# Weights through SyncE's queue in 2 KB rows, with staging and casts, in place of a software DMA that casts

## The chip, the cores and the metric

One core of one Trainium2 chip. The metric is the device time of one execution in microseconds (us); the kernel before has a median of 257.8 us (3 runs, 257.32 to 258.01). Ratios are of one kernel's fast runs over the other's fast runs of the same rounds, so they are not quite the ratio of the medians that are quoted. A profile's span is about 1.8 us shorter than the time of the same run (258.8 for 260.65).

## The reference

Attention with 16 query heads and 4 key heads, and then a gated MLP with a spatial mix; 8 batches of 384 positions.

```python
scores = (q @ k^T) / sqrt(64);  attn = softmax(scores);  x = attn @ v   # x: 8 x 384 x 1024
h = max(x @ w_in, 0)                       # w_in: 1024 x 1024 float32
u, v = h[..., :512], h[..., 512:]
v_n = (v - mean(v)) / sqrt(var(v) + 1e-6)
v_s = w_spatial @ v_n + b_spatial          # w_spatial ~ 0.01/384, b_spatial = 1
out = (u * v_s) @ w_out                    # w_out: 512 x 1024 float32
```

The weights are shared by all batches: they are read once, while the first batch is worked on.

## The kernel before

The kernel is a list of steps (`FIRST` for batches 0 to 2, `STEADY`, `LAST`), and every engine runs its steps in the order of the list. In the code, `S` is a product of scores, `E` its exponential, `X` the product with v, `V` the product x @ w_in for the half v, `G,..,gu` the same for the half u, `Tw` the transposes of w_spatial, `cq`/`ck`/`cv`/`cws` casts of loaded data to 16 bits (last letter: v = VectorE, s = ScalarE, p = GpSimd), and `dk`/`dq` DMA transposes.

Row `32*g + r` of `w_in16` and of `xT` holds feature `256*g + 32*kc + r`, because the program lets the X products of each group g of heads write to their own 32 partitions (128\*32 in the page's line of X). This layout matters below. Weights are loaded by a software DMA from GpSimd, which casts on the way (in the trace each w_in load writes 256 KB for its 512 KB of float32):

```python
def load_w_in(part, g):                                   # eight of these, 512 KB of float32 each
    c0, c1 = part * DH, (part + 1) * DH
    nc.gpsimd.dma_start(
        w_in16[32 * g : 32 * (g + 1), :, c0:c1],
        moe_w_in[g * G * D : (g + 1) * G * D, c0:c1].rearrange("(kc r) n -> r kc n", r=32),
    )

def load_w_out(h):                                        # two of these
    nc.gpsimd.dma_start(w_out16[:, 2 * h : 2 * h + 2, :], ...)

def v_mm(b, st, k0=0, k1=NKT):                            # "V": needs all eight kc of w_in
    for kc in range(k0, k1):
        nc.tensor.matmul(held["pv", b, st], xT[b][:, kc, st * P : (st + 1) * P],
                         w_in16[:, kc, DH:DFF], start=(kc == 0), stop=(kc == NKT - 1))
# ... all loads of q, k, v and w_spatial: nc.sync.dma_start with the 128 partitions outermost
```

The softmax here doesn't subtract the row's maximum and nothing guards it: scores larger than these inputs give would overflow.

Of the kernel before, what the change touches and what calls it, by code (L numbers as in the profile page):

```python
# [17 lines left out]

FIRST = """
lk,0,0,2 lq,0,0,0,1,s cq,0,0,0,1,0,v ck,0,0,s Tk,0,0 cq,0,0,0,1,1,s lk,0,2,4 Tq,0,0,0 lq,0,1,0,1  # L20
lq,0,0,1,3 lq,0,1,1,3 cq,0,1,0,1,1,p tq,0,0,0,v tk,0,0,s S,0 cq,0,1,0,1,0,v ck,0,1,v E,0 S,0
lwi,0,1,3 cq,0,0,1,3,0,p lwi,0,1,0 cq,0,1,1,3,0,p Tk,0,1 lk,1 lv,0 Tq,0,1,0 tk,0,1,v tq,0,1,0,v S,0
lq,1,0 cq,0,0,1,3,1,v E,0 E,0 lq,1,1 S,0 Tq,0,0,1 S,0 S,0 Tq,0,0,2 cq,0,1,1,3,1,p tq,0,0,1,v
Tq,0,1,1 tq,0,1,1,v S,0 ck,1,1,p tq,0,0,2,v E,0 lwi,0,1,2 lwi,0,1,1 ck,1,0,p S,0 E,0 cv,0,p E,0
X,0,0,2 S,0 lv,1 lws,0 Tq,0,1,2 S,0 S,0 lbi,0 Tkk,1 rv,0,0 E,0 lk,2 S,0 X,0,0,0 X,0,0,1 lq,2,0
lq,2,1 E,0 cq,1,0,0,1,1,p E,0 E,0 E,0 S,0 cq,1,0,1,3,0,p cq,1,0,1,3,1,p cq,1,0,0,1,0,p tq,0,1,2,v
tkk,1,v cq,1,1,0,1,0,p S,0 E,0 xm,0,0,1 X,0,1,2 xm,0,0,0 X,0,1,0 X,0,1,1 S,0 S,0 V,0,0,0,4 V,0,0,4,8
rv,0,1 S,0 S,0 E,0 E,0 E,0 E,0 cq,1,1,0,1,1,s xm,0,1,0 xm,0,1,1 Tqq,1,0 tqq,1,0,0,v V,0,1,0,4
ru,0,0,v cq,1,1,1,3,0,v tqq,1,0,1,v cv,1,v E,0 E,0 S,0 S,0 E,0 X,0,2,0 X,0,2,2 X,0,2,1 lwi,0,0,2
cws,0,0 cws,0,2 cq,1,1,1,3,1,p cws,0,1 lwi,0,0,0 lwo,0,1 cq,2,0,0,3,0,p lwi,0,0,3 lwi,0,0,1  # L30
cq,2,0,0,3,1,p cq,2,1,0,3,0,p ck,2,1,p lwo,0,0 ck,2,0,p cq,2,1,0,3,1,p E,0 rl,0,2 S,0 re,0,2 E,0 S,0
xm,0,2,1 Tqq,1,1 E,0 xm,0,2,0 V,0,1,4,8 Tw,0,0,2 Tw,0,2,3 S,0 S,0 tqq,1,1,0,s ru,0,1,v tw,0,0,2
V,0,2,0,4 V,0,2,4,8 bs,0,0 bs,0,1 ru,0,2,v tqq,1,1,1,v E,0 tw,0,2,3 bs,0,2 S,0 E,0 E,0 S,0 X,1,0,2
rl,1,0 X,1,0,0 X,1,0,1 Tqq,1,2 S,0 re,1,0 S,0 xm,1,0,0 xm,1,0,1 V,1,0,0,4 E,0 dq,2,0 dk,2 V,1,0,4,8
S,0 rs,0 tqq,1,2,0,v nm,0,2 E,0 tqq,1,2,1,v nm,0,0 nm,0,1 ru,1,0,v G,0,gs,0,0,0,1 S,0 G,0,gs,2,0,0,1
dq,2,1 lq,3,1 lk,3 E,0 mk,0,gs,0,v G,0,gs,0,1,0,1 S,0 lv,2 lq,3,0 mk,0,gs,2,v G,0,gs,2,1,0,1 E,0 E,0
sa,0,0 sa,0,1 sa,0,2 sa,0,3 S,0 cq,3,1,0,3,1,p cq,3,1,0,3,0,p X,1,1,2 cq,3,0,0,3,0,p cq,3,0,0,3,1,p
X,1,1,1 X,1,1,0 E,0 rl,1,1 re,1,1 ck,3,0,p xm,1,1,0 xm,1,1,1 G,0,gu,0,0,0 S,0 G,0,gu,0,0,1 E,0 S,0
mk,0,gu,0,v G,0,gu,2,0,0 S,0 E,0 E,0 G,0,gu,0,1,0 S,0 G,0,gu,2,0,1 S,0 G,0,gu,0,1,1 mk,0,gu,2,v E,0
E,0 E,0 bs,1,0 G,0,gu,2,1,0 S,0 G,0,gu,2,1,1 S,0 gt,0,0 E,0 X,1,2,0 gt,0,2 gt,0,3 gt,0,1 X,1,2,2  # L40
cv,2,v E,0 S,0 S,0 V,1,1,0,4 rl,1,2 V,1,1,4,8 S,0 G,0,go,0,0,0 G,0,go,0,0,1 mk,0,go,0,v S,0 re,1,2
E,0 E,0 G,0,go,0,1,0 E,0 G,0,go,0,1,1 S,0 E,0 xm,1,2,0 oc,0,1,v oc,0,0,v E,0 X,2,0,2 X,1,2,1 rl,2,0
xm,1,2,1 re,2,0 ru,1,1,s X,2,0,0 X,2,0,1 S,0 S,0 xm,2,0,0 G,1,w12,2,0,0 G,1,w12,2,0,1 S,0 S,0
ck,3,1,s E,0 E,0 mk,1,w12,2,v xm,2,0,1 G,1,w12,2,1,0 bs,1,1 G,1,w12,2,1,1 oc,0,2,v ru,1,2,v oc,0,3,v
E,0 bs,1,2 E,0 X,2,1,2 rl,2,1 re,2,1 X,2,1,0 dq,3,0 S,0 xm,2,1,0 G,2,w24,0,0,0 E,0 lq,4,0
G,2,w24,0,0,1 S,0 lv,3 dk,3 lq,4,1 rs,1 st,0,0 mk,2,w24,0,p nm,1,0 dq,3,1 nm,1,1 X,2,1,1 S,0
G,2,w24,0,1,0 E,0 S,0 xm,2,1,1 E,0 oc,0,4,v G,2,w24,0,1,1 nm,1,2 E,0 G,1,gs,0,0,0,1 S,0 cv,3,p
mk,1,gs,0,p ru,2,0,s oc,0,5,v S,0 G,1,gs,2,0,0,1 mk,1,gs,2,v E,0 G,1,gs,0,1,0,1 G,1,gs,2,1,0,1 S,0
E,0 S,0 sa,1,0 sa,1,2 sa,1,1 E,0 E,0 sa,1,3 G,1,gu,0,0,0 G,1,gu,0,0,1 S,0 E,0 mk,1,gu,0,p
G,1,gu,2,0,0 S,0 G,1,gu,2,0,1 S,0 G,1,gu,0,1,0 S,0 E,0 mk,1,gu,2,p G,1,gu,2,1,0 S,0 G,1,gu,0,1,1 E,0  # L50
gt,1,1 gt,1,0 S,0 G,1,gu,2,1,1 E,0 X,2,2,2 E,0 rl,2,2 E,0 gt,1,3 gt,1,2 X,2,2,1 S,0 G,2,w10,1,0,0
G,2,w10,1,0,1 S,0 E,0 S,0 re,2,2 E,0 mk,2,w10,1,v xm,2,2,1 bs,2,0 G,2,w10,1,1,0 G,2,w10,1,1,1
oc,1,0,v oc,1,1,v ru,2,1,v X,2,2,0 xm,2,2,0 bs,2,1 lv,4 st,1,0 lk,4 st,0,1 st,0,2 E,0
# [716 lines left out]
```

## Time and profile before

| | before |
|---|---|
| time, median | 257.8 us |
| span of the profiled run | 258.8 us (its time was 260.65 us) |
| TensorE busy | 242.5 us, 94% |
| first V product starts | 26.91 us |
| first u product starts | 53.12 us |

From the page of the kernel before: engine PE (TensorE) with busy us, share and instructions; then three lines over the span in 40 slices (6.5 us each), busy tenths of PE, granted clock of PE in tenths, and mean busy tenths of the DMA engines (9 stands for 90% or more); then two DMA queues with packets, MB and their share of the time of 16 engines (q1 is SyncE's queue, q0 the software DMA).

```profile
...
PE 242.5 (94%) x2505; PEld 124.1 (48%) x2505; DVE 152.1 (59%) x287; ACT 182.8 (71%) x229; POOL 45.3 (18%) x92
...
PE   2985899899999999999999999999999999999993
...
PEclk9999599999999999999999999999999999999999
DMA  7999999894994008995394909293582011300606
...
q1 hardware_dynamic: 53648, 37.75, 54.3%
q0 software_dynamic: 2720, 3.15, 8.0%
...
```

From the sixth slice on PE is at 9 tenths, but for an 8 in the eighth slice and the end of the program. The large dips are in the first five slices. There the DMA engines are at 7 and then 9 tenths, slice after slice: the start is short of data, the rest is short of TensorE.

From the waits of PE, kernel before (who waited <- for whom: us in total, times, longest; "pk" and "pq" are the transposes of k and q on TensorE, "sc" the scores, "pv" and "pu" the V and u products):

```profile
...
PE pv L441 <- DMA w_in<-in_moe_w_in_dram: 4.2, 1, 4.2
PE pk L314 <- ACT k L306: 4.2, 1, 4.2
...
```

And from PE's timeline (start us, duration, engine, line, operation, output<-inputs, count, and the idle time ahead of it with its releaser):

```profile
...
22.09 0.60 PE L378 MATMUL sc<-qT,kT 64*128 64x512 f16 x4
26.91 3.57 PE L441 MATMUL pv<-w_in,xt 128*128 128x512 f16 x8 [4.21 <-DMA w_in<-in_moe_w_in_dram]
...
39.17 1.90 PE L441 MATMUL pv<-w_in,xt 128*128 128x512 f16 x8
...
53.12 0.82 PE L616 MATMUL pu<-xt,w_in 64*128 64x384 f16 x8
...
```

The wait of 4.2 us for k is the start itself: PE's first product starts at 4.18 us, when the first load is in and cast. The eight products of the first V (26.91 us) waited 4.21 us for w_in. They then took 3.57 us, at a granted clock of 0.50; the same eight at 39.17 us took 1.90, at 1.00. With the slow products the pause is worth about 6 us (an estimate: 4.21 + 3.57 - 1.90), and this is what the change is after.

### The profile page before, as it was taken

The numbers are of one execution on the slowest core, as the hardware profiler recorded it, in microseconds if no ns is written. First come the engines' busy times: TensorE is split into PE (matmuls) and PEld (weight loads), VectorE is DVE, ScalarE is ACT, GpSimd is POOL, SyncE is SP. The second block draws the span as 40 slices with busy tenths as digits, with TensorE's granted clock in tenths as the row PEclk, the third lists the DMA queues.
The fourth block names the chain that finished last, engine by engine and source line by source line (L and its number), as shares of the span: only waits on it lengthen the run. The fifth ranks groups of instructions, "written<-read, shape, count | busy, mean of one in ns | idle before, by whom it ended". The sixth has DMA issues, their size and how long they took to land.

```text
span 258.8 us, 5938 instructions
## 1 busy us (share of the span) xinstructions
PE 242.5 (94%) x2505; PEld 124.1 (48%) x2505; DVE 152.1 (59%) x287; ACT 182.8 (71%) x229; POOL 45.3 (18%) x92
## 2 busy tenths in 40 slices
PE   2985899899999999999999999999999999999993
...
PEclk9999599999999999999999999999999999999999
DMA  7999999894994008995394909293582011300606
GB/s 183 230 265 247 292 196 195 153 286 125 237 262 102 4 3 304 165 345 174 113 205 131 313 8 233 95 323 114 104 214 84 3 55 61 127 6 0 243 0 243
DMA packets 57578, 41.66 MB, mean 161 GB/s; under 512 B 26832, under 2 KB 53840, under 8 KB 57552
## 3 DMA queue, kind: packets, MB, share of 16 engines
q1 hardware_dynamic: 53648, 37.75, 54.3%
q0 software_dynamic: 2720, 3.15, 8.0%
...
## 4 chain that ended last, share of the span: by engine, by line
PE 83%; DMA 9%; DVE 4%; ACT 1%; POOL 0%; issue 0%; SPq 0%; ACTq 0%
PE X L398 18%; PE po L643 14%; PE pu L616 12%; PE sc L378 11%; PE pv L603 11%; PE pv L441 5%; DMA w_in<-in_moe_w_in_dram 4%; PE po L548 4%; PE pu L513 4%; PE psp L629 3%; DMA k<-in_k_dram 3%; DMA q<-in_q_dram 2%; DVE v_s L499 1%; DVE v_n L473 1%; PE psp L487 1%; ACT aT L389 1%
## 5 line engine op out<-in xcount | busy, mean ns | idle before, releaser
L389 ACT ACTIVATE aT<-sc 128x1024 f16<-128x1024 f32 x144 | 140.8, 1023 | 35.7 <-PE sc L378 35.3
L643 PE MATMUL po<-w_out,gT 64*128 64x512 f16 x288 | 68.0, 376 | 0.0
L603 PE MATMUL pv<-w_in,xt 64*128 64x512 f16 x272 | 64.9, 376 | 0.0
L378 PE MATMUL sc<-qT,kT 64*128 64x512 f16 x288 | 56.4, 396 | 1.4 <-DVE qT L308 0.5
L427 DVE TENSOR_TENSOR xt<-X,rec 128x512 f16<-128x512 f32 x48 | 31.2, 686 | 13.4 <-ACT rec L415 4.8
L308 DVE COPY osb<-po 128x512 f32<-128x512 f32 x39 | 26.6, 686 | 17.8 <-PE po L643 15.3
L616 PE MATMUL pu<-xt,w_in 64*128 64x384 f16 x384 | 36.7, 323 | 0.0
L398 PE MATMUL X<-aT,v 128*32 128x512 f16 x576 | 35.9, 379 | 0.0
L643 PEld LDWEIGHTS <-gT 64*128 64x128 f16 x288 | 25.4, 94 | 14.5 <-DVE mark_v L697 3.0
L603 PEld LDWEIGHTS <-xt 64*128 64x128 f16 x272 | 24.8, 94 | 12.5 <-issue 3.8
L308 POOL CAST q<-q 128x768 f16<-128x768 f32 (+2 forms) x34 | 24.4, 747 | 35.8 <-DMA q<-in_q_dram 33.2
L525 DVE SCALAR_TENSOR_TENSOR gT<-pu,v_s 128x384 f16<-128x384 f32 x31 | 16.1, 553 | 24.6 <-PE pu L616 20.9
L378 PEld LDWEIGHTS <-kT 64*128 64x128 f16 x288 | 17.1, 94 | 25.2 <-issue 16.9
L616 PEld LDWEIGHTS <-w_in 64*128 64x128 f16 x384 | 20.0, 94 | 13.3 <-issue 0.8
L499 DVE TENSOR_TENSOR v_s<-psp,bias_b 128x384 f32<-128x384 f32 x32 | 20.0, 688 | 5.6 <-PE psp L487 3.4
L398 PEld LDWEIGHTS <-v 128*32 128x32 f16 x576 | 15.9, 96 | 15.5 <-issue 1.6
L398 PE MATMUL X<-aT,ones 128*32 128x512 f16 x288 | 20.6, 392 | 0.5 <-DVE v_s L499 0.2
L409 ACT ACTIVATE rec<-X 128x512 f32<-128x512 f32 x22 | 13.1, 598 | 11.1 <-PE X L398 11.1
L462 DVE BATCH_NORM_STATS2 stats<-v_r 128x6 f32<-128x512 f32 x24 | 16.5, 686 | 5.6 <-ACT v_r L454 2.9
L699 POOL MEMSET mark_p<- 1x1 f32 x20 | 1.8, 88 | 101.4 <-PE psp L629 57.7
L441 PE MATMUL pv<-w_in,xt 128*128 128x512 f16 x56 | 15.3, 419 | 4.2 <-DMA w_in<-in_moe_w_in_dram 4.2
L629 PE MATMUL psp<-wsT,v_n 64*128 64x384 f16 x144 | 15.5, 323 | 0.9 <-DVE v_n L473 0.8
...
## 6 DMA issues: line engine op xcount, KB each, us to landing
...
```

The source lines that it names most:

```text
L308: engine.tensor_copy(dst, src)
L378: mm = nc.tensor.matmul(sc[:, half, :], kT[b][lo:hi, gp, t, :], rhs[lo:hi, :], start=True, stop=True)
L389: nc.scalar.activation(aT[b, qt][:, gp, t], held["sc", b, u], AF.Exp, scale=scale)
L398: nc.tensor.matmul(dst[32 * g : 32 * (g + 1), :], v16[:, g, t, 32 * part : 32 * (part + 1)] if part < 2 else ones32, a[:, g // 2, t, g % 2 ...
L427: nc.vector.tensor_tensor(xt[:, jj, :, qt * P : (qt + 1) * P], held["X", b, qt, jj].rearrange("p (j q) -> p j q", j=G), held["rec", b, qt] ...
L441: nc.tensor.matmul(held["pv", b, st], xT[b][:, kc, st * P : (st + 1) * P], w_in16[:, kc, DH:DFF], start=(kc == 0), stop=(kc == NKT - 1),)
L462: nc.vector.bn_stats(s6, held["v_r", b, st])
L499: nc.vector.tensor_tensor(held["v_s", b][:, m, :].rearrange("p (t s) -> p t s", t=NST), held["psp", b, m][:, 0:S].rearrange("p (t s) -> p ...
L603: yield lambda kc=kc: nc.tensor.matmul(held["pv", b, st], xT[b][rows, kc, st * P : (st + 1) * P], w_in16[rows, kc, DH:DFF], start=(first a ...
L616: yield lambda kc=kc: nc.tensor.matmul(held["pu", b, mu][:, 0:S], w_in16[rows, kc, mu * P : (mu + 1) * P], xT[b][rows, kc, :], start=(firs ...
L629: yield lambda st=st: nc.tensor.matmul(held["psp", b, m][:, 0:S], held["v_n", b, st][rows, m * P : (m + 1) * P], wsT16[rows, st, :], start ...
L643: yield lambda m=m: nc.tensor.matmul(held["po", b, i], held["gT", b][rows, m, tt * P : (tt + 1) * P], w_out16[rows, m, half * 512 : (half ...
```

## The change

The intent: load the weights as float32 through SyncE's hardware queue, in rows of 2 KB, into five small staging buffers, cast them on GpSimd and others, and leave the software DMA out. The steps of `FIRST` are put into a new order for it; `STEADY` and `LAST` stay.

```diff
-    def load_w_in(part, g):        # ... software DMA, 8 x 512 KB
-    def load_w_out(h):             # ... software DMA, 2 x 1 MB
+    def load_w(part, i):
+        piece = stage.tile([P, 512], FP32, name=f"w32_{part}_{i}", tag="w32", bufs=5)
+        if part < 2:
+            src = moe_w_in.rearrange("(g kc r) n -> kc g r n", g=HKV, kc=NKT)[
+                i, :, :, part * DH : (part + 1) * DH
+            ]
+        else:
+            m, half = i // 2, i % 2
+            src = moe_w_out[m * P : (m + 1) * P, half * 512 : (half + 1) * 512]
+        nc.sync.dma_start(piece, src)
+        loaded["w32", part, i] = piece
+
+    def cast_w(part, i, engine):
+        # ... copy(w_in16[:, i, cols] or w_out16[:, m, cols], loaded["w32", part, i], engine)
 FIRST = ...
-  lwi,0,1,3 ... lwi,0,1,0 ... lwi,0,1,2 lwi,0,1,1 ...            (on GpSimd)
+  lw,0,1,4 lw,0,1,3 lw,0,1,2 lk,1 lv,0 lw,0,1,1 lw,0,1,0 lq,1,1 lq,1,0 lw,0,1,5 lw,0,1,6 lw,0,1,7 ...   (on SyncE)
+  cw,0,1,4,p ... cw,0,1,3,s ... cw,0,1,7,p ... cw,0,1,5,v ...    (24 casts)
```

The helpers for transposes and casts get arguments for parts of a tile that this version does not use, and transposes that were done for two head groups at once are done one by one. The number of TensorE instructions is the same (2505 products).

More of the change, by code (lines that the diff above doesn't have):

```diff
@@ L16 @@
 DVE, ACT = mybir.EngineType.DVE, mybir.EngineType.Activation
+SPLIT = 0
 FIRST = """
-lk,0,0,2 lq,0,0,0,1,s cq,0,0,0,1,0,v ck,0,0,s Tk,0,0 cq,0,0,0,1,1,s lk,0,2,4 Tq,0,0,0 lq,0,1,0,1
-lq,0,0,1,3 lq,0,1,1,3 cq,0,1,0,1,1,p tq,0,0,0,v tk,0,0,s S,0 cq,0,1,0,1,0,v ck,0,1,v E,0 S,0
-lwi,0,1,3 cq,0,0,1,3,0,p lwi,0,1,0 cq,0,1,1,3,0,p Tk,0,1 lk,1 lv,0 Tq,0,1,0 tk,0,1,v tq,0,1,0,v S,0
-lq,1,0 cq,0,0,1,3,1,v E,0 E,0 lq,1,1 S,0 Tq,0,0,1 S,0 S,0 Tq,0,0,2 cq,0,1,1,3,1,p tq,0,0,1,v
-Tq,0,1,1 tq,0,1,1,v S,0 ck,1,1,p tq,0,0,2,v E,0 lwi,0,1,2 lwi,0,1,1 ck,1,0,p S,0 E,0 cv,0,p E,0
@@ L25 @@
-X,0,0,2 S,0 lv,1 lws,0 Tq,0,1,2 S,0 S,0 lbi,0 Tkk,1 rv,0,0 E,0 lk,2 S,0 X,0,0,0 X,0,0,1 lq,2,0
-lq,2,1 E,0 cq,1,0,0,1,1,p E,0 E,0 E,0 S,0 cq,1,0,1,3,0,p cq,1,0,1,3,1,p cq,1,0,0,1,0,p tq,0,1,2,v
-tkk,1,v cq,1,1,0,1,0,p S,0 E,0 xm,0,0,1 X,0,1,2 xm,0,0,0 X,0,1,0 X,0,1,1 S,0 S,0 V,0,0,0,4 V,0,0,4,8
-rv,0,1 S,0 S,0 E,0 E,0 E,0 E,0 cq,1,1,0,1,1,s xm,0,1,0 xm,0,1,1 Tqq,1,0 tqq,1,0,0,v V,0,1,0,4
-ru,0,0,v cq,1,1,1,3,0,v tqq,1,0,1,v cv,1,v E,0 E,0 S,0 S,0 E,0 X,0,2,0 X,0,2,2 X,0,2,1 lwi,0,0,2
-cws,0,0 cws,0,2 cq,1,1,1,3,1,p cws,0,1 lwi,0,0,0 lwo,0,1 cq,2,0,0,3,0,p lwi,0,0,3 lwi,0,0,1
@@ L31 @@
-cq,2,0,0,3,1,p cq,2,1,0,3,0,p ck,2,1,p lwo,0,0 ck,2,0,p cq,2,1,0,3,1,p E,0 rl,0,2 S,0 re,0,2 E,0 S,0
-xm,0,2,1 Tqq,1,1 E,0 xm,0,2,0 V,0,1,4,8 Tw,0,0,2 Tw,0,2,3 S,0 S,0 tqq,1,1,0,s ru,0,1,v tw,0,0,2
-V,0,2,0,4 V,0,2,4,8 bs,0,0 bs,0,1 ru,0,2,v tqq,1,1,1,v E,0 tw,0,2,3 bs,0,2 S,0 E,0 E,0 S,0 X,1,0,2
-rl,1,0 X,1,0,0 X,1,0,1 Tqq,1,2 S,0 re,1,0 S,0 xm,1,0,0 xm,1,0,1 V,1,0,0,4 E,0 dq,2,0 dk,2 V,1,0,4,8
-S,0 rs,0 tqq,1,2,0,v nm,0,2 E,0 tqq,1,2,1,v nm,0,0 nm,0,1 ru,1,0,v G,0,gs,0,0,0,1 S,0 G,0,gs,2,0,0,1
@@ L36 @@
-dq,2,1 lq,3,1 lk,3 E,0 mk,0,gs,0,v G,0,gs,0,1,0,1 S,0 lv,2 lq,3,0 mk,0,gs,2,v G,0,gs,2,1,0,1 E,0 E,0
-sa,0,0 sa,0,1 sa,0,2 sa,0,3 S,0 cq,3,1,0,3,1,p cq,3,1,0,3,0,p X,1,1,2 cq,3,0,0,3,0,p cq,3,0,0,3,1,p
-X,1,1,1 X,1,1,0 E,0 rl,1,1 re,1,1 ck,3,0,p xm,1,1,0 xm,1,1,1 G,0,gu,0,0,0 S,0 G,0,gu,0,0,1 E,0 S,0
-mk,0,gu,0,v G,0,gu,2,0,0 S,0 E,0 E,0 G,0,gu,0,1,0 S,0 G,0,gu,2,0,1 S,0 G,0,gu,0,1,1 mk,0,gu,2,v E,0
-E,0 E,0 bs,1,0 G,0,gu,2,1,0 S,0 G,0,gu,2,1,1 S,0 gt,0,0 E,0 X,1,2,0 gt,0,2 gt,0,3 gt,0,1 X,1,2,2
@@ L41 @@
-cv,2,v E,0 S,0 S,0 V,1,1,0,4 rl,1,2 V,1,1,4,8 S,0 G,0,go,0,0,0 G,0,go,0,0,1 mk,0,go,0,v S,0 re,1,2
-E,0 E,0 G,0,go,0,1,0 E,0 G,0,go,0,1,1 S,0 E,0 xm,1,2,0 oc,0,1,v oc,0,0,v E,0 X,2,0,2 X,1,2,1 rl,2,0
-xm,1,2,1 re,2,0 ru,1,1,s X,2,0,0 X,2,0,1 S,0 S,0 xm,2,0,0 G,1,w12,2,0,0 G,1,w12,2,0,1 S,0 S,0
-ck,3,1,s E,0 E,0 mk,1,w12,2,v xm,2,0,1 G,1,w12,2,1,0 bs,1,1 G,1,w12,2,1,1 oc,0,2,v ru,1,2,v oc,0,3,v
-E,0 bs,1,2 E,0 X,2,1,2 rl,2,1 re,2,1 X,2,1,0 dq,3,0 S,0 xm,2,1,0 G,2,w24,0,0,0 E,0 lq,4,0
-G,2,w24,0,0,1 S,0 lv,3 dk,3 lq,4,1 rs,1 st,0,0 mk,2,w24,0,p nm,1,0 dq,3,1 nm,1,1 X,2,1,1 S,0
@@ L47 @@
-G,2,w24,0,1,0 E,0 S,0 xm,2,1,1 E,0 oc,0,4,v G,2,w24,0,1,1 nm,1,2 E,0 G,1,gs,0,0,0,1 S,0 cv,3,p
-mk,1,gs,0,p ru,2,0,s oc,0,5,v S,0 G,1,gs,2,0,0,1 mk,1,gs,2,v E,0 G,1,gs,0,1,0,1 G,1,gs,2,1,0,1 S,0
-E,0 S,0 sa,1,0 sa,1,2 sa,1,1 E,0 E,0 sa,1,3 G,1,gu,0,0,0 G,1,gu,0,0,1 S,0 E,0 mk,1,gu,0,p
-G,1,gu,2,0,0 S,0 G,1,gu,2,0,1 S,0 G,1,gu,0,1,0 S,0 E,0 mk,1,gu,2,p G,1,gu,2,1,0 S,0 G,1,gu,0,1,1 E,0
-gt,1,1 gt,1,0 S,0 G,1,gu,2,1,1 E,0 X,2,2,2 E,0 rl,2,2 E,0 gt,1,3 gt,1,2 X,2,2,1 S,0 G,2,w10,1,0,0
-G,2,w10,1,0,1 S,0 E,0 S,0 re,2,2 E,0 mk,2,w10,1,v xm,2,2,1 bs,2,0 G,2,w10,1,1,0 G,2,w10,1,1,1
@@ L53 @@
-oc,1,0,v oc,1,1,v ru,2,1,v X,2,2,0 xm,2,2,0 bs,2,1 lv,4 st,1,0 lk,4 st,0,1 st,0,2 E,0
+lq,0,0,0,1,0,1,s lk,0,0,2 lq,0,1,0,1 lk,0,2,4 cq,0,0,0,1,1,0,1,p lq,0,0,1,3 lq,0,1,1,3
+cq,0,1,0,1,1,0,1,p lw,0,1,4 cq,0,1,0,1,0,0,1,p cq,0,0,0,1,0,0,1,v lw,0,1,3 lw,0,1,2 lk,1 lv,0
+ck,0,0,0,3,s lw,0,1,1 lw,0,1,0 lq,1,1 cq,0,1,1,3,0,0,1,p cq,0,1,1,3,1,0,1,p lq,1,0 lw,0,1,5 lw,0,1,6
+Tk,0,0,0,3 Tq,0,0,0,0,1 tq,0,0,0,0,1,v ck,0,1,0,3,v tk,0,0,0,3,s lw,0,1,7 S,0 S,0 lv,1 lws,0
+Tk,0,1,0,3 Tq,0,1,0,0,1 E,0 tk,0,1,0,3,v S,0 tq,0,1,0,0,1,v S,0 S,0 E,0 E,0 lw,0,0,4 lw,0,0,3
@@ new lines @@
+lw,0,0,1 lw,0,0,2 lw,0,0,0 lk,2 lw,0,0,6 E,0 cq,0,0,1,3,0,0,1,v E,0 lq,2,0 cq,0,0,1,3,1,0,1,v
+Tq,0,0,1,0,1 lbi,0 lw,0,0,7 lw,0,2,0 lq,2,1 lw,0,0,5 S,0 Tq,0,1,2,0,1 cw,0,1,4,p cv,0,p ck,1,0,0,3,p
+E,0 tq,0,0,1,0,1,v cw,0,1,1,p cw,0,1,0,p Tq,0,1,1,0,1 cw,0,1,3,s S,0 tq,0,1,1,0,1,v S,0 X,0,0,2 S,0
+E,0 tq,0,1,2,0,1,s S,0 Tq,0,0,2,0,1 S,0 Tk,1,0,0,3 rv,0,0 tq,0,0,2,0,1,v S,0 E,0 X,0,0,0 cw,0,1,2,p
+cq,1,1,0,1,1,0,1,p ck,1,1,0,3,p cq,1,0,1,3,1,0,1,p cq,1,1,0,1,0,0,1,p cq,1,0,1,3,0,0,1,p cw,0,1,7,p
@@ new lines @@
+cws,0,0 cw,0,0,1,p E,0 E,0 S,0 E,0 E,0 E,0 X,0,1,2 cv,1,p S,0 xm,0,0,0 cq,1,1,1,3,0,0,1,v X,0,0,1
+ck,2,1,0,3,p cw,0,0,3,p X,0,1,0 rl,0,1 E,0 ck,2,0,0,3,p xm,0,0,1 cq,1,1,1,3,1,0,1,v cw,0,0,4,p
+cws,0,2 S,0 cws,0,1 S,0 X,0,1,1 re,0,1 xm,0,1,0 cq,2,0,0,3,1,0,1,p cw,0,0,7,p cq,2,0,0,3,0,0,1,p
+cw,0,0,6,p xm,0,1,1 cq,2,1,0,3,0,0,1,p cw,0,0,5,p cq,2,1,0,3,1,0,1,p cw,0,1,5,v cq,1,0,0,1,0,0,1,v
+E,0 E,0 tk,1,0,0,3,s cq,1,0,0,1,1,0,1,v cw,0,1,6,v V,0,0,0,4 Tk,1,1,0,3 S,0 S,0 tk,1,1,0,3,s E,0
+Tq,1,1,0,0,1 Tq,1,1,1,0,1 Tq,1,0,0,0,1 tq,1,0,0,0,1,v V,0,0,4,8 E,0 Tq,1,1,2,0,1 S,0 tq,1,1,1,0,1,v
@@ new lines @@
+tq,1,1,0,0,1,v tq,1,1,2,0,1,v S,0 X,0,2,1 X,0,2,2 X,0,2,0 E,0 E,0 rl,0,2 S,0 ru,0,0,v S,0 re,0,2
+V,0,1,0,4 Tq,1,0,1,0,1 E,0 xm,0,2,0 xm,0,2,1 E,0 tq,1,0,1,0,1,v bs,0,0 V,0,1,4,8 S,0 S,0 cw,0,0,0,v
+V,0,2,0,4 V,0,2,4,8 ru,0,1,s S,0 E,0 S,0 E,0 X,1,0,2 E,0 bs,0,1 rl,1,0 re,1,0 X,1,0,0 X,1,0,1
+cw,0,0,2,v ru,0,2,v bs,0,2 Tw,0,0,2 Tq,1,0,2,0,1 E,0 rs,0 xm,1,0,1 xm,1,0,0 S,0 tq,1,0,2,0,1,s E,0
+S,0 E,0 Tw,0,2,3 V,1,0,0,4 V,1,0,4,8 nm,0,2 tw,0,0,2 nm,0,0 S,0 tw,0,2,3 nm,0,1 ru,1,0,v
+G,0,gs,2,0,0,1 S,0 lw,0,2,1 lw,0,2,4 dk,2 G,0,gs,0,0,0,1 dq,2,0 lw,0,2,2 dq,2,1 lw,0,2,6 lw,0,2,5
@@ new lines @@
+lw,0,2,3 lv,2 lw,0,2,7 lk,3 mk,0,gs,2,v cw,0,2,0,v mk,0,gs,0,v G,0,gs,2,1,0,1 S,0 G,0,gs,0,1,0,1 S,0
+sa,0,3 E,0 E,0 X,1,1,2 E,0 sa,0,1 sa,0,2 sa,0,0 lq,3,0 lq,3,1 E,0 rl,1,1 X,1,1,1 X,1,1,0 S,0
+G,0,gu,2,0,0 S,0 G,0,gu,2,0,1 re,1,1 xm,1,1,1 xm,1,1,0 mk,0,gu,2,v E,0 cw,0,2,2,v cw,0,2,1,p S,0
+G,0,gu,0,0,0 S,0 G,0,gu,0,0,1 S,0 mk,0,gu,0,v cw,0,2,4,p cw,0,2,6,p cw,0,2,5,p G,0,gu,2,1,0 S,0
+G,0,gu,0,1,0 S,0 E,0 G,0,gu,0,1,1 E,0 E,0 S,0 G,0,gu,2,1,1 S,0 E,0 E,0 E,0 gt,0,1 gt,0,3 gt,0,0
+gt,0,2 X,1,2,2 X,1,2,1 E,0 rl,1,2 E,0 V,1,1,0,4 re,1,2 cw,0,2,3,v bs,1,0 cw,0,2,7,p xm,1,2,1
@@ new lines @@
+ck,3,0,0,3,v V,1,1,4,8 S,0 ru,1,1,s E,0 ck,3,1,0,3,p cv,2,p cq,3,0,0,3,0,0,1,p cq,3,0,0,3,1,0,1,p
+G,0,go,0,0,0 cq,3,1,0,3,0,0,1,p cq,3,1,0,3,1,0,1,p S,0 G,0,go,0,0,1 X,1,2,0 X,2,0,2 dq,3,1 dk,3
+dq,3,0 mk,0,go,0,v E,0 rl,2,0 xm,1,2,0 S,0 G,0,go,0,1,0 S,0 G,0,go,0,1,1 X,2,0,0 X,2,0,1 re,2,0 E,0
+oc,0,0,v xm,2,0,0 oc,0,1,s E,0 S,0 G,1,w12,2,0,0 G,1,w12,2,0,1 E,0 S,0 E,0 mk,1,w12,2,v S,0
+G,1,w12,2,1,0 G,1,w12,2,1,1 E,0 xm,2,0,1 oc,0,2,v X,2,1,2 X,2,1,1 oc,0,3,v bs,1,1 ru,1,2,s bs,1,2
+rl,2,1 S,0 E,0 G,2,w24,0,0,0 G,2,w24,0,0,1 re,2,1 rs,1 S,0 mk,2,w24,0,v xm,2,1,1 E,0 S,0
@@ new lines @@
+G,2,w24,0,1,0 X,2,1,0 E,0 oc,0,4,s S,0 nm,1,2 nm,1,0 nm,1,1 E,0 xm,2,1,0 G,2,w24,0,1,1
+G,1,gs,0,0,0,1 S,0 oc,0,5,v mk,1,gs,0,v S,0 ru,2,0,s G,1,gs,0,1,0,1 E,0 E,0 G,1,gs,2,0,0,1 sa,1,0
+mk,1,gs,2,v sa,1,1 S,0 G,1,gs,2,1,0,1 G,1,gu,0,0,0 S,0 G,1,gu,0,0,1 sa,1,2 sa,1,3 E,0 G,1,gu,2,0,0
+S,0 mk,1,gu,0,v E,0 G,1,gu,2,0,1 S,0 G,1,gu,0,1,0 S,0 E,0 G,1,gu,0,1,1 S,0 mk,1,gu,2,p E,0
+G,1,gu,2,1,0 S,0 E,0 gt,1,0 G,1,gu,2,1,1 S,0 X,2,2,2 E,0 E,0 gt,1,1 gt,1,3 gt,1,2 X,2,2,0 S,0 rl,2,2
+E,0 E,0 re,2,2 G,2,w10,1,0,0 G,2,w10,1,0,1 S,0 lv,3 st,0,2 E,0 mk,2,w10,1,v S,0 G,2,w10,1,1,0
@@ L54 @@
+xm,2,2,0 bs,2,0 oc,1,0,v G,2,w10,1,1,1 ru,2,1,v oc,1,1,v X,2,2,1 lq,4,0 lq,4,1 E,0 lv,4 st,0,1
+st,0,0 lk,4 bs,2,1 st,1,0 xm,2,2,1 cv,3,p
 """
 STEADY = """
-X,0,0,2 rl,0,0 re,0,0 X,0,0,0 X,0,0,1 S,0 E,0 xm,0,0,0 xm,0,0,1 ck,1,0,p ck,1,1,p cq,1,0,0,3,0,p
-cq,1,0,0,3,1,p cq,1,1,0,3,0,p cq,1,1,0,3,1,p cv,1,p dk,1 dq,1,0 dq,1,1 G,-1,w12,2,0,0 G,-1,w12,2,0,1
-mk,-1,w12,2,v S,0 E,0 S,0 E,0 G,-1,w12,2,1,0 oc,-2,2,v G,-1,w12,2,1,1 ru,-1,2,v oc,-2,3,v st,-2,1
-bs,-1,2 X,0,1,2 rl,0,1 re,0,1 X,0,1,0 X,0,1,1 rs,-1 S,0 E,0 xm,0,1,0 xm,0,1,1 nm,-1,0 nm,-1,1
@@ L61 @@
-G,0,w24,0,0,0 G,0,w24,0,0,1 mk,0,w24,0,v nm,-1,2 S,0 E,0 S,0 E,0 G,0,w24,0,1,0 oc,-2,4,v
-G,0,w24,0,1,1 ru,0,0,s oc,-2,5,v st,-2,2 bs,0,0 lk,2 lq,2,0 lq,2,1 lv,2 S,0 E,0 G,-1,gs,0,0,0,1
-mk,-1,gs,0,p S,0 E,0 G,-1,gs,2,0,0,1 mk,-1,gs,2,p G,-1,gs,0,1,0,1 sa,-1,0 sa,-1,1 S,0 E,0
-G,-1,gs,2,1,0,1 sa,-1,2 sa,-1,3 X,0,2,2 rl,0,2 re,0,2 X,0,2,0 X,0,2,1 S,0 E,0 xm,0,2,0 xm,0,2,1
-G,-1,gu,0,0,0 G,-1,gu,0,0,1 mk,-1,gu,0,p S,0 E,0 G,-1,gu,2,0,0 G,-1,gu,2,0,1 mk,-1,gu,2,p S,0 E,0
-G,-1,gu,0,1,0 G,-1,gu,0,1,1 gt,-1,0 gt,-1,1 S,0 E,0 G,-1,gu,2,1,0 G,-1,gu,2,1,1 gt,-1,2 gt,-1,3 S,0
@@ L67 @@
-E,0 S,0 E,0 G,0,w10,1,0,0 G,0,w10,1,0,1 mk,0,w10,1,v S,0 E,0 S,0 E,0 G,0,w10,1,1,0 oc,-1,0,v
-G,0,w10,1,1,1 ru,0,1,v oc,-1,1,v st,-1,0 bs,0,1 S,0 E,0
+X,0,0,2 rl,0,0 re,0,0 X,0,0,0 X,0,0,1 S,0 E,0 xm,0,0,0 xm,0,0,1 ck,1,0,0,3,p ck,1,1,0,3,p
+cq,1,0,0,3,0,0,1,p cq,1,0,0,3,1,0,1,p cq,1,1,0,3,0,0,1,p cq,1,1,0,3,1,0,1,p cv,1,p dk,1 dq,1,0
+dq,1,1 G,-1,w12,2,0,0 G,-1,w12,2,0,1 mk,-1,w12,2,v S,0 E,0 S,0 E,0 G,-1,w12,2,1,0 oc,-2,2,v
+G,-1,w12,2,1,1 ru,-1,2,v oc,-2,3,v st,-2,1 bs,-1,2 X,0,1,2 rl,0,1 re,0,1 X,0,1,0 X,0,1,1 rs,-1 S,0
@@ new lines @@
+E,0 xm,0,1,0 xm,0,1,1 nm,-1,0 nm,-1,1 G,0,w24,0,0,0 G,0,w24,0,0,1 mk,0,w24,0,v nm,-1,2 S,0 E,0 S,0
+E,0 G,0,w24,0,1,0 oc,-2,4,v G,0,w24,0,1,1 ru,0,0,s oc,-2,5,v st,-2,2 bs,0,0 lk,2 lq,2,0 lq,2,1 lv,2
+S,0 E,0 G,-1,gs,0,0,0,1 mk,-1,gs,0,p S,0 E,0 G,-1,gs,2,0,0,1 mk,-1,gs,2,p G,-1,gs,0,1,0,1 sa,-1,0
+sa,-1,1 S,0 E,0 G,-1,gs,2,1,0,1 sa,-1,2 sa,-1,3 X,0,2,2 rl,0,2 re,0,2 X,0,2,0 X,0,2,1 S,0 E,0
+xm,0,2,0 xm,0,2,1 G,-1,gu,0,0,0 G,-1,gu,0,0,1 mk,-1,gu,0,p S,0 E,0 G,-1,gu,2,0,0 G,-1,gu,2,0,1
+mk,-1,gu,2,p S,0 E,0 G,-1,gu,0,1,0 G,-1,gu,0,1,1 gt,-1,0 gt,-1,1 S,0 E,0 G,-1,gu,2,1,0 G,-1,gu,2,1,1
@@ L69 @@
+gt,-1,2 gt,-1,3 S,0 E,0 S,0 E,0 G,0,w10,1,0,0 G,0,w10,1,0,1 mk,0,w10,1,v S,0 E,0 S,0 E,0
+G,0,w10,1,1,0 oc,-1,0,v G,0,w10,1,1,1 ru,0,1,v oc,-1,1,v st,-1,0 bs,0,1 S,0 E,0
 """
@@ L204, in load_v, with load_q @@
         loaded["v32", b] = v32
-    def load_q(b, gp, t0=0, t1=NST, queue=None):
+    def load_q(b, gp, t0=0, t1=NST, j0=0, js=1, queue=None):
         if ("q32", b, gp) not in loaded:
@@ L210, in load_q @@
         (queue or nc.sync).dma_start(
-            loaded["q32", b, gp][:, :, t0 * D : t1 * D],
-            q[b, h0 : h0 + 2 * G].rearrange("h (p t) d -> p h (t d)", t=NST)[
+            loaded["q32", b, gp][:, j0::js, t0 * D : t1 * D],
+            q[b, h0 + j0 : h0 + 2 * G : js].rearrange("h (p t) d -> p h (t d)", t=NST)[
                 :, :, t0 * D : t1 * D
@@ L215, in load_q, with cast_k @@
         )
-    def cast_k(b, gp, engine):
+    def cast_k(b, gp, t0, t1, engine):
         if ("k16", b) not in loaded:
@@ L220, in cast_k @@
         k32 = loaded["k32", b].rearrange("p (gp h) (t d) -> p gp t h d", gp=NGP, t=NST)
-        copy(loaded["k16", b][:, gp], k32[:, gp], engine)
+        copy(loaded["k16", b][:, gp, t0:t1], k32[:, gp, t0:t1], engine)
     def cast_v(b, engine):
@@ L226, in cast_v, with cast_q @@
         loaded["v16", b] = v16
-    def cast_q(b, gp, t0, t1, half, engine):
+    def cast_q(b, gp, t0, t1, half, j0, js, engine):
         if ("q16", b, gp) not in loaded:
@@ L232, in cast_q @@
             )
-        dst = loaded["q16", b, gp][:, t0:t1, :, half, :]
-        src = loaded["q32", b, gp][:, half * G : (half + 1) * G, :].rearrange(
+        dst = loaded["q16", b, gp][:, t0:t1, j0::js, half, :]
+        src = loaded["q32", b, gp][:, half * G + j0 : (half + 1) * G : js, :].rearrange(
             "p j (t d) -> p t j d", t=NST
@@ L237, in cast_q @@
         copy(dst, src, engine)
-    def load_w_in(part, g):
-        c0, c1 = part * DH, (part + 1) * DH
-        nc.gpsimd.dma_start(
-            w_in16[32 * g : 32 * (g + 1), :, c0:c1],
-            moe_w_in[g * G * D : (g + 1) * G * D, c0:c1].rearrange("(kc r) n -> r kc n", r=32),
-        )
-    def load_w_out(h):
-        nc.gpsimd.dma_start(
-            w_out16[:, 2 * h : 2 * h + 2, :],
-            moe_w_out[2 * h * P : (2 * h + 2) * P, :].rearrange("(m p) n -> p m n", p=P),
-        )
+    def load_w(part, i):
[10 more added lines that the diff above has]
+    def cast_w(part, i, engine):
+        if part < 2:
+            dst = w_in16[:, i, part * DH : (part + 1) * DH]
+        else:
+            m, half = i // 2, i % 2
+            dst = w_out16[:, m, half * 512 : (half + 1) * 512]
+        copy(dst, loaded["w32", part, i], engine)
     def load_ws():
```

104 lines of the change are left out of this document (46 added, 58 removed).

## The prediction

> **What bounds it now.** TensorE: the page's first part has PE busy 242.5 of 258.8 us (94%), the chain of waits is 83% PE. About 16 us are idle, nearly all before 27 us: 4.18 before the first transpose, some waits of 0.5, and 4.21 before the first V product at 26.91 us, "PE pv <- DMA w_in" in the waits view. Those eight products took 3.57 us, later ones 1.90 (timeline), so the stall cost about 6 us. From batch 3 on the change leaves the program alone. DMA is full for the first 45 us (slice line: 7999999).
>
> **Removed, added, moved.** Ten software DMAs go (8.0% of 16 engines = 20.7 us of all sixteen; 110 ns per 2 KB of fp32). 24 pieces of 256 KB come in 2 KB rows; hardware packets of 2 KB took about 85 ns in the packet records, so 3072 are 16 us if spread over 16 engines. 24 casts of 128x512 come, about 0.6 us each, mostly on GpSimd (18% busy): harmless. PE's work is the same (2505 matmuls), re-ordered.
>
> **What decides it.** A w_in piece is read by a pattern whose outermost dimension is 4, then 32 rows, then 512 columns; other loads have 128 outermost. [...] Then each piece is 32 packets x 85 ns = 2.7 us on the same four engines, and every load behind it finishes only when its share on those four has.
>
> My sum for those four (estimate, packet medians: 256 B 18 ns, 512 B 32, 768 B 36, 2 KB 85): q and k of batch 0 done at 9.5 us, three pieces 17.7, k1 and v0 20, two pieces 25.4, q1 30, the last three V pieces 38, cast about 40. The second half of the first V product ends near 42 us instead of 30.5. Five u pieces until 54.5, k2 56; piece 0,6 waits for a staging buffer whose cast on GpSimd stands behind k2's; the rest of u and q2 come by 75.5, so the first u product starts near 76 us instead of 53.1. Nothing gives it back, since PE is full: +23 us.
>
> With 16 engines V's pieces land near 24 us and the stall mostly goes: 252 to 257 us.
>
> **Prediction: 280 us, 254 to 291 (8 in 10).** Faster by over 2%: 0.10; within 2%: 0.15; slower by over 2%: 0.75.
>
> **What would show it.**
> - SyncE's queue has 56,912 packets if w_in pieces use 4 engines (4 semaphore packets each), 57,104 if 16.
> - w_in pieces take 10 us and more from issue to landing; mean DMA busy share before 75 us falls to about 5 tenths, though loads are late.
> - PE idles about 12 us before the second half of the first V product and 10 us more before the first u product.
> - From the first u product on both kernels take the same time, within 2 us.
> - If V starts near 25 us without that idle time, my step on four engines is wrong.
>
> **What would make it wrong.** The split goes by the destination's 128 partitions; four engines run faster alone than my packet times; the wait for the staging buffer (GpSimd's order, SyncE's queue blocked in order) is longer or shorter than summed, by up to 10 us.

The number of four engines was the author's assumption. The sum: first u product at 76 us in place of 53.1, so +23 us, on the median of 257.8, given as 280. That each engine of a DMA adds one semaphore packet was assumed too; experiment 1 tests both.

## The result, and the profile after

The changed kernel takes 288.1 us (median of 4 runs, 287.54 to 289.14), the kernel before in the same rounds 257.9; the ratio is 1.117 (95% interval 1.113 to 1.122). The result is correct.

The page of the changed kernel, the same lines (slices of 7.1 us):

```profile
...
PE 248.9 (87%) x2505; PEld 125.9 (44%) x2505; DVE 148.1 (52%) x292; ACT 187.1 (65%) x236; POOL 49.8 (17%) x96
...
PE   2947727917969999999999999999999999999994
...
PEclk9999975975999999999999999999999999999999
DMA  8749552287799497957664966466657101110415
...
q1 hardware_dynamic: 56912, 44.05, 57.2%
...
```

Before 86 us PE has now nine slices that are not full, and its granted clock falls in four of the first ten (to 7, 5, 7 and 5 tenths). The DMA engines are, on average over the 16, about half idle or more from 29 to 57 us (5, 5, 2, 2 tenths) although PE waits for data. From 86 us on PE is full, as before. SyncE's queue has exactly 56,912 packets.

The waits of PE, changed kernel:

```profile
...
PE psw L293 <- POOL ws L283: 8.4, 1, 8.4
PE sc L368 <- ACT aT L381: 4.6, 4, 3.3
PE pk L334 <- ACT k L326: 4.2, 1, 4.2
PE pv L438 <- DVE w_in L328: 2.4, 1, 2.4
PE pq L349 <- DVE q L328: 2.4, 1, 2.4
PE pv L438 <- POOL w_in L328: 2.3, 1, 2.3
PE pk L334 <- POOL k L328: 2.0, 1, 2.0
PE pu L613 <- POOL w_in L328: 1.8, 1, 1.8
...
```

PE's timeline, changed kernel:

```profile
...
32.80 1.04 PE L438 MATMUL pv<-w_in,xt 128*128 128x512 f16 x4 [1.07 <-DVE xt L424]
...
38.51 0.60 PE L438 MATMUL pv<-w_in,xt 128*128 128x512 f16 x2
41.47 0.58 PE L438 MATMUL pv<-w_in,xt 128*128 128x512 f16 x1 [2.37 <-DVE w_in L328]
44.34 0.58 PE L438 MATMUL pv<-w_in,xt 128*128 128x512 f16 x1 [2.28 <-POOL w_in L328]
...
57.70 0.23 PE L293 MATMUL psw<-ident,ws 128*128 128x128 f16 x1
66.38 0.71 PE L293 MATMUL psw<-ident,ws 128*128 128x128 f16 x5 [8.45 <-POOL ws L283]
...
68.72 2.77 PE L438 MATMUL pv<-w_in,xt 128*128 128x512 f16 x8
...
77.15 0.81 PE L613 MATMUL pu<-xt,w_in 64*128 64x384 f16 x8
...
```

The first V product is split by the new order. Its first half starts at 32.80 us, and its last two chunks wait 2.37 and 2.28 us for casts of w_in; the eighth starts at 44.34 us. The first u product starts at 77.15 us. The largest single wait, 8.45 us, shows up between the two, on the transposes of w_spatial ("psw"), and is put down to GpSimd.

The first profile of the kernel before came from a run above the median, so it was profiled once more (run before_again, below: one run, at the median). Against that one (span 255.4 us), the changed kernel is later by:

| PE event | before_again | changed | later by |
|---|---|---|---|
| eighth product of the first V starts | 27.3 us | 44.3 us | 17.0 us |
| first u product starts | 48.7 us | 77.1 us | 28.4 us |
| first product with w_out starts | 60.2 us | 90.9 us | 30.7 us |
| 241st product with w_out starts | 203.0 us | 233.6 us | 30.6 us |
| end | 255.4 us | 285.8 us | 30.4 us |

All is lost before 91 us; from there on the two are alike. The 30.4 us have two parts. PE is idle for 36.9 us (285.8 - 248.9) in place of 14.1 (its page has 241.3 busy): 22.8 us more. And the same 2505 products keep it busy 7.6 us longer. Part of this is the clock: from 39.8 to 50.0 and from 60.3 to 70.5 us the granted clock is 0.50 and PE busy for 10.4 us, in before_again it is 0.50 for 3.4 us only. By these figures the slower clock is worth about 3.5 us (an estimate, half of the 7 us more, as eight V products took 3.57 us at 0.50 and 1.90 at 1.00); the rest of the 7.6 was not taken apart.

### The profile page after: what moved, and what is told of

The parts are those of the page before. It is cut to its first block, busy times and chain, and to the rows that moved or that the text cites. A ratio compares the mean times of both kernels' runs of the same rounds, so it can differ in the third digit from the quotient of the medians.

```text
span 285.8 us, 5979 instructions
## 1 busy us (share of the span) xinstructions
PE 248.9 (87%) x2505; PEld 125.9 (44%) x2505; DVE 148.1 (52%) x292; ACT 187.1 (65%) x236; POOL 49.8 (17%) x96
## 3 DMA queue, kind: packets, MB, share of 16 engines
q1 hardware_dynamic: 56912, 44.05, 57.2%
## 4 chain that ended last, share of the span: by engine, by line
PE 64%; DMA 21%; SPq 4%; issue 3%; POOL 3%; DVE 2%; ACT 1%; POOLq 0%; ACTq 0%; DVEq 0%
PE X L395 13%; PE po L640 12%; DMA w<-in_moe_w_in_dram 10%; PE pv L600 9%; PE pu L613 9%; PE sc L368 8%; DMA ws<-in_moe_w_spatial_dram 5%; DMA k<-in_k_dram 4%; PE po L545 3%; PE pu L510 3%; PE psp L626 3%; SPq L213 2%; SPq L261 2%; DMA q<-in_q_dram 1%; POOL w_in L328 1%
## 5 line engine op out<-in xcount | busy, mean ns | idle before, releaser
L368 PE MATMUL sc<-qT,kT 64*128 64x512 f16 x288 | 57.6, 407 | 5.5 <-ACT aT L381 4.6
L395 PE MATMUL X<-aT,v 128*32 128x512 f16 x576 | 38.7, 399 | 0.0
L328 DVE COPY osb<-po 128x512 f32<-128x512 f32 x37 | 25.5, 688 | 19.2 <-PE po L640 16.3
L328 POOL CAST q<-q 128x768 f16<-128x768 f32 (+2 forms) x33 | 23.7, 746 | 15.8 <-DMA q<-in_q_dram 14.0
L395 PE MATMUL X<-aT,ones 128*32 128x512 f16 x288 | 21.9, 413 | 0.5 <-DVE v_s L496 0.2
L406 ACT ACTIVATE rec<-X 128x512 f32<-128x512 f32 x23 | 13.7, 597 | 11.5 <-PE X L395 11.5
```

Source lines behind the costliest of these rows:

```text
L328: engine.tensor_copy(dst, src)
L368: nc.tensor.matmul(sc[:, half, 0 : 512 // js], kT[b][lo:hi, gp, t, :], qT[b, gp][lo:hi, qt, j0::js], start=True, stop=True,)
L395: nc.tensor.matmul(dst[32 * g : 32 * (g + 1), :], v16[:, g, t, 32 * part : 32 * (part + 1)] if part < 2 else ones32, a[:, g // 2, t, g % 2 ...
```

## The experiments

### 1. Only the outermost dimension: 16, 8 and 2 groups in place of 4

The one-line edit. It takes other rows of w_in, so the result is wrong; the bytes, the 2 KB rows, the number of DMAs, the staging, the casts, the waits and the order of steps are the same. The places of the rows in DRAM do change with it.

```diff
-            src = moe_w_in.rearrange("(g kc r) n -> kc g r n", g=HKV, kc=NKT)[    # 4 groups of 32 rows
+            src = moe_w_in.rearrange("(g kc r) n -> kc g r n", g=16, kc=NKT)[     # 16 groups of 8 rows
```

> The changed kernel, only the rows that a w_in piece takes are others: 16 groups of 8 rows, in place of 4 groups of 32 (wrong result on purpose; same bytes, 2 KB rows, pieces, casts, waits and order). Theory (number of DMA engines is set by the outermost dimension): 57,104 packets on SyncE's queue in place of 56,912, no wait of over 1.5 us of PE before the first V product's second half nor before the spatial transposes, first u product within 2 us of 53, time 252 to 258 us. Rivals (five staging pieces with SyncE's queue blocked in order; cast order on GpSimd; the hardware queue or fp32 rows slower than the software DMA; the new order of steps): nothing of theirs is changed, so 286 to 290 us.

> As outer16 but 8 groups of 16 rows (wrong result on purpose). Theory: 56,976 packets (8 semaphore packets each for 16 pieces), pieces need 16 x 85 ns on 8 engines; first V product's second half ends near 31 us, u pieces by about 53 us, time 256 to 264 us. Rivals: 286 to 290 us.

> As outer16 but 2 groups of 64 rows (wrong result on purpose). Theory: 56,880 packets, each piece 64 x 85 ns = 5.4 us on two engines; first V product ends near 64 us, first u product near 119 us, time 318 to 345 us. Rivals: 286 to 290 us.

Measured (the packets are those of SyncE's queue; "in flight" is the mean number of 2 KB packets under way at once, over the first 1,024 of them in the packet records while any was; the median with 8 groups is of all four runs, its three fast ones having 269.6; 2 groups ran twice):

| groups | packets | in flight | GB/s of these | eighth V product | first u product | time, median | ratio to before |
|---|---|---|---|---|---|---|---|
| 2 | 56,880 | 2.07 | 46 | 62.6 us | 113.8 us | 325.0 us | 1.259 (1.251 to 1.266) |
| 4 (the change) | 56,912 | 4.00 | 76 | 44.3 us | 77.1 us | 288.1 us | 1.117 |
| 8 | 56,976 | 7.89 | 118 | 35.3 us | 61.4 us | 270.6 us | 1.046 (1.040 to 1.053) |
| 16 | 57,104 | 11.65 | 184 | 28.2 us | 53.4 us | 259.9 us | 1.006 (1.001 to 1.010) |

The queue lines of the pages with 2, 8 and 16 groups:

```profile
...
q1 hardware_dynamic: 56880, 44.05, 50.5%
...
```

```profile
...
q1 hardware_dynamic: 56976, 44.05, 61.7%
...
```

```profile
...
q1 hardware_dynamic: 57104, 44.05, 63.4%
...
```

The packet counts are those expected, each to the packet: with 2, 4, 8 and 16 groups the 16 DMAs of w_in add 32, 64, 128 and 256 packets to the 56,848 of the rest, so each adds as many as there are groups. (In the packet records of the changed kernel they are packets of 4 bytes; the document calls them semaphore packets.) As many packets of data are in flight as there are groups. The records do not name a packet's engine; both counts are read here as the number of engines that a DMA runs on. With 16 groups the mean is 11.65 only, but the most frequent number is 16 there too, as it is 2, 4 and 8 in the others; why it is often less was not taken apart. A packet itself did not get faster with more groups: the medians of the same 1,024 packets are 87, 91, 147 and 129 ns with 2, 4, 8 and 16 groups. So the gain is not that the rows' new places in DRAM made packets cheaper; more of them ran at once. The rivals (five staging buffers, cast order, hardware queue, new order of steps) are the same in all four kernels and expected 286 to 290 us in each. They fall as causes of the 28 us between 4 and 16 groups.

Not all went as expected. With 8 groups 256 to 264 us were expected and 270.6 measured, with 16 groups 252 to 258 and 259.9. With 8 groups the first V product already ended at 35.9 us where 31 was expected; the sum had 85 ns for a packet, and 147 were measured. With 16 groups V was in time, and a wait that the sum had left out came after it (with 8 groups it is 3.9 us). The waits of PE with 16 groups:

```profile
...
PE psw L293 <- POOL ws L283: 3.2, 1, 3.2
...
PE pv L438 <- DVE w_in L328: 0.8, 1, 0.8
PE pv L438 <- POOL w_in L328: 0.7, 1, 0.7
...
```

PE's timeline with 16 groups:

```profile
...
42.34 0.71 PE L293 MATMUL psw<-ident,ws 128*128 128x128 f16 x5 [3.22 <-POOL ws L283]
...
44.68 3.59 PE L438 MATMUL pv<-w_in,xt 128*128 128x512 f16 x8
...
53.40 0.81 PE L613 MATMUL pu<-xt,w_in 64*128 64x384 f16 x8
```

V no longer waits for long (0.8 and 0.7 us), but the transposes of w_spatial wait 3.22 us, and the V products after them take 3.59 us in place of 1.90 (granted clock 0.52; the page has 6 and 7 tenths in its two slices from 38.8 to 51.7 us). GpSimd casts w_spatial in the order of the list, behind a cast of k of batch 2, for whose load it waits 4.05 us; SyncE issues that load only at 34.7 us, behind five w_in pieces. The stall moved.

### 2. V's half with 16 groups, u's half with 4

```diff
-   rearrange(..., g=HKV, kc=NKT)
+   rearrange(..., g=16 if part == 1 else HKV, kc=NKT)
```

> V's half of w_in with 16 groups of 8 rows (wrong result on purpose), u's half with 4 groups as in the change. Theory: 57,008 packets, the first V product is not late (second half ends before 33 us), the u pieces are (last one cast about 58 to 61 us), time 260 to 268 us: so of the loss of 30 us a part belongs to each half. Rivals: 286 to 290 us.

Measured: 270.8 us, ratio 1.049 (1.044 to 1.054), 57,008 packets; the eighth V product starts at 27.5 us, the first u product at 60.0. Of the 28.2 us between 4 and 16 groups (288.1 - 259.9), V's half, changed first, makes 17.3 (288.1 - 270.8) and u's half 10.9. The time lies 3 us above the expected range: 9.3 us of PE's waits are again at the w_spatial transposes. (This run counts as correct though V's rows are wrong: in this data v enters through w_spatial, which is about 0.01/384, beside a bias of 1, so the comparison cannot see it.)

### 3. Is the largest wait the cost? GpSimd's order, with 4 and with 16 groups

```diff
-ck,2,1,0,3,p cw,0,0,3,p ... ck,2,0,0,3,p ... cw,0,0,4,p
-cws,0,2 S,0 cws,0,1 S,0
+cws,0,2 cws,0,1 cw,0,0,3,p ... cw,0,0,4,p
+ck,2,1,0,3,p S,0 ck,2,0,0,3,p S,0
```

> The changed kernel (4 groups, correct result), only GpSimd's order is other: the two last casts of w_spatial and two casts of u pieces now come before the two casts of k of batch 2. In the changed kernel the largest single wait of PE, 8.4 us before the spatial transposes, was put down to GpSimd. Theory (four engines deliver too late; the wait only shows where the order puts it): that wait goes, but PE then waits for the u pieces, so the time stays at 283 to 289 us. Rival (GpSimd's order, not the loads, costs this part): 8 us or more are gained, 277 to 280 us.

> The same order of GpSimd with 16 groups of 8 rows (wrong result on purpose). Where 16 engines deliver, the 3.2 us before the spatial transposes are GpSimd's order, and the products after it run at half the clock (3.6 in place of 1.9 us): expected 253 to 257 us, 3 to 5 us under the kernel with 16 groups alone (259.9). If the wait moves elsewhere, it stays at 258 to 260.

With 4 groups: 286.9 us, correct, ratio 1.116 (1.109 to 1.122). The largest wait of the changed kernel's profile is gone, and 1.2 us of 8.4 are gained by the medians, less by the ratios (1.117 and 1.116, each against runs of the kernel before in the same rounds). Its waits of PE begin:

```profile
...
PE sc L368 <- ACT aT L381: 5.5, 5, 3.7
PE pq L349 <- DVE v_r L449: 5.4, 1, 5.4
...
```

The new wait of 5.4 us is on VectorE, and VectorE's timeline shows what it stood behind, the cast of a u piece that waited 8.16 us for its load:

```profile
...
60.67 0.43 DVE L328 CAST w_in<-w 128x512 f16<-128x512 f32 x1 [8.16 <-DMA w<-in_moe_w_in_dram]
...
```

So PE waits for the u pieces, as expected, though by way of VectorE. The first u product starts at 76.2 us in place of 77.1. With 4 groups the data are late, and the order of casts only decides on which instruction the wait is booked.

With 16 groups: 259.0 us (258.01 to 259.98), ratio 1.007 (1.001 to 1.013). Expected were 253 to 257, a miss; the other outcome that was named, a wait that moves and 258 to 260 us, came true. By the ratio nothing was gained (outer16 has 1.006). The mechanism did work locally: the first u product starts at 48.7 us in place of 53.4 us (outer16's profile is of a run slightly above its median, order16's of its fastest, so this is somewhat flattered). But the first product with w_out starts at 61.7 in place of 64.0 us: half was given back between, to waits that were not there:

```profile
...
PE pu L613 <- DVE mark_v L694: 0.8, 1, 0.8
...
PE sc L368 <- DMA qT<-q: 0.7, 1, 0.7
...
PE pu L613 <- POOL w_in L328: 0.4, 1, 0.4
...
```

They are for a u piece, for the DMA transpose of q of batch 2, and for a mark (a one-element write that orders the steps), which VectorE does right after a cast whose w_out piece it waited 3.94 us for: the next loads in SyncE's queue.

### 4. A correct kernel on 16 engines

One DMA brings the 32 partitions of one group for two chunks: 32 rows outermost, 2 KB rows, 128 KB.

```diff
-        piece = stage.tile([P, 512], FP32, ..., bufs=5)
-        nc.sync.dma_start(piece, src)
+        piece = stage.tile([P, 2, 512], FP32, ..., bufs=3)
+        rows = moe_w_in.rearrange("(g kc r) n -> g r kc n", g=HKV, kc=NKT)
+        for g in range(HKV):
+            nc.sync.dma_start(piece[32 * g : 32 * (g + 1)],
+                              rows[g, :, 2 * i : 2 * i + 2, part * DH : (part + 1) * DH])
# w_out in rows of 4 KB; r_pool bufs 3 -> 2; order of the list as in 3
```

> A correct version with 16 engines: the outermost dimension is 32 rows of one group; a DMA brings 32 partitions x 2 chunks x 2 KB (128 KB), 32 DMAs for w_in in place of 16, three staging buffers of 4 KB in place of five of 2 KB (reciprocal buffers 3 to 2 to make room), w_out in 4 KB rows, GpSimd's order as in order16. Theory: 254 to 262 us, 16 more issues of about 0.5 us on SyncE being the only new cost, every w_in DMA with 16 semaphore packets. Rivals that blame the hardware queue, the fp32 staging or the casts: over 280 us.

Measured: 261.8 us, correct, ratio 1.018 (1.012 to 1.024), unclear against before at 2%. 56,784 packets: 2,560 of data and 36 weight DMAs with 16 semaphore packets each above the 53,648 of before's queue, as many each as with 16 groups, so all are read as running on 16 engines. It is 26 us faster than the change with the same queue, float32 and casts, and still not faster than the kernel before.

### 5. The kernel before again, and with V's weights issued earlier

> The kernel before, profiled once more, since its first profile fell in a run of 260.65 us, above its median of 257.8: a span near 256 us, the first V product near 25 us instead of 26.9, everything from the first u product on as in the first profile (153 us from there to the first output product of the last but one batch).

Measured: 257.24 us, span 255.4. Its first V product and its first u product:

```profile
...
24.97 2.97 PE L441 MATMUL pv<-w_in,xt 128*128 128x512 f16 x8 [2.84 <-DMA w_in<-in_moe_w_in_dram]
...
48.72 0.82 PE L616 MATMUL pu<-xt,w_in 64*128 64x384 f16 x8
...
```

The stall was 2.84 us here and 4.21 in the first profile: the start of the kernel varies from run to run. Slow products followed the shorter pause too: 2.97 us for eight (granted clock 1.00 for the first 0.6 us, then 0.50), after 2.84 us here, as 3.57 after 4.21 us, and in outer16 3.59 for eight V products that began 2.3 us after a pause of 3.22. The first u product starts at 48.7 us here and at 53.1 in the first profile, and 1.0 us of these 4.4 is given back by the end (spans 255.4 and 258.8). From the first u product to the 241st product with w_out it takes 154.3 us, in the first profile 153.3.

```diff
-ck,1,1,p tq,0,0,2,v E,0 lwi,0,1,2 lwi,0,1,1 ck,1,0,p
+lwi,0,1,2 lwi,0,1,1 ck,1,1,p tq,0,0,2,v E,0 ck,1,0,p
```

> The kernel before, only GpSimd's order is other: the last two software DMAs of V's weights are issued ahead of the two casts of k of batch 1, for whose load GpSimd waited 3.9 us. If the 4.2 us of PE before the first V product are that order, and not the software DMA's speed, they fall to under 2 us and the time to 253 to 256 us. If the DMA engines' bandwidth is the limit (they are busy all the time), the same bytes ahead of V's weights or behind change only which load is late: 256 to 259 us.

Measured: 261.7 us median of 6 runs, 255.98 to 262.6; five of the six count as slow, being over 1.5% above the fastest, so there is no verdict on the time. This experiment is inconclusive there. Its profile, of a slow run, still shows one thing: the wait before V is gone (V starts at 22.2 us and the first u product at 46.1), and PE has a wait that is 0.5 us in before_again:

```profile
...
PE sc L378 <- DMA kT<-k: 4.9, 1, 4.9
...
```

PE waits 4.9 us for the DMA transpose of k of batch 2. That would fit a start that is bound by all the bytes it needs, where V's weights ahead make others late; with one slow profile it is not shown.

## Why the prediction was right, point by point

- **Four engines: right.** The runs agree: 56,912 packets as forecast, 4.00 packets in flight on average, and 2, 4, 8 and 16 groups give 325.0, 288.1, 270.6 and 259.9 us. Other numbers of groups were not run.
- **Every load behind is held up: right, and more directly than said.** SyncE itself is held in the instruction that issues: 4.12 us for the load of v. The changed kernel's timeline of SyncE (start, duration of the issue):

```profile
...
8.07 0.63 SPq L206 DMA_DIRECT2D k<-in_k_dram  x1
8.75 4.12 SPq L213 DMA_DIRECT2D v<-in_v_dram  x1
12.90 4.63 SPq L261 DMA_DIRECT2D w<-in_moe_w_in_dram  x2
17.64 6.86 SPq L220 DMA_DIRECT2D q<-in_q_dram  x2
...
```

With 16 groups, the same instructions:

```profile
...
8.03 0.46 SPq L206 DMA_DIRECT2D k<-in_k_dram  x1
8.53 0.51 SPq L213 DMA_DIRECT2D v<-in_v_dram  x1
9.08 1.19 SPq L261 DMA_DIRECT2D w<-in_moe_w_in_dram  x2
11.71 2.41 SPq L220 DMA_DIRECT2D q<-in_q_dram  x2
...
```

The load of v, whose own pattern is the same in both, takes SyncE 4.12 us to issue behind w_in pieces of 4 groups and 0.51 behind pieces of 16. GpSimd's cast of v, which waits for that load (7.87 and 4.00 us), starts at 22.24 and at 16.25 us.

- **The sum for the four engines: right within 4 us, point for point.** Forecast and measured: v0 in at 20 us, cast at 22.2; last V piece cast at about 40, at 43.7; first V product ends near 42, at 44.9; first u product near 76, at 77.1.
- **The time, 280 forecast and 288.1 measured: in the range, 8 us low; the step was the base.** The +23 were the first u product at 76 in place of "53.1 us", which comes from a profile of a 260.65 us run; they were then added to 257.8, the median. In the one profile of a run near the median that product starts at 48.7 us. So the mis-sized term is the start of before, by 4.4 us. Another 1.1 us is in the sum (77.1 for 76), and 2.0 more come after the first u product (30.4 - 28.4), where "within 2 us" is just met against before_again and fails against the first profile, by which it is 2.9: PE waits 1.8 us for the u piece that is cast last, and some tenths behind it. The range of 254 to 291 us was so wide that it held the time of the kernel before too; the credit is for the mechanism and the shift, not for the range.
- **Idle before V and before u: right in sum, wrong in place for the second.** PE is idle for 20.7 us of the first 45 us (busy 24.3), in before_again for 8.7 of the first 26.9 (busy 18.2): 12 us more, as forecast. From there to the first u product it is idle for 8.8 us, in before_again for 0.1, where 10 more were forecast; but this second wait came at the transposes of w_spatial, 8.45 us, ahead of the u product. Experiment 3 with 4 groups shows that it is the same lateness.
- **Issue to landing of 10 us: cannot be told.** The profile leaves this column empty for w_in pieces. **DMA busy at about 5 tenths before 75 us: near;** weighted over four stretches up to 77 us it is 0.60.
- **"252 to 257 us" with 16 engines: wrong,** 259.9 and, with a better order, 259.0. The sum looked at V's wait alone, and had 85 ns for a packet that then took 129 (median of the first 1,024 in outer16). The 85 ns are those of the 128 packets of 2 KB at the end of the kernel before. Its software DMA, cast and all, took 98 ns for as much of w_in (median; mean 110), so in these runs the hardware queue was not the faster one for w_in, packet by packet. Once V's pieces are early, the casts of w_spatial, then u's pieces and batch 2's transposes are what is late.
- **"Harmless" casts: right as far as it was tested.** outer16 has all 24 casts and counts as the same as before at 2% (1.006); pairs has them too and is unclear (1.018).
